# Pass one of a fused attention and two-layer kernel: block writes placed behind the raw loads, a third staging buffer, and a bank of its own for one product

## The chip, the cores and the metric

One core of one Trainium2 chip runs the whole program. The metric is device time in microseconds, from one launch. Engines are named as the profile names them: PE is TensorE (PEld its weight loads), DVE is VectorE, ACT is ScalarE, POOL is GpSimd, and SP is SyncE, which here only issues transfers (SPq).

## What is computed

Block-causal attention feeds a first feed-forward layer, whose output, after an RMS norm, feeds a gated second one.

```python
x = attention(q, k, v)              # 4 x 8 heads x 576 x 64 -> 2304 x 512
h = x @ w_in                        # 512 x 2048
x = (h - tanh(h)) @ w_out           # 2048 x 512
rms = sqrt(mean(x * x, -1) + 1e-06)
xn = x / rms * rms_g
g, val = xn @ w_gate, xn @ w_val    # 512 x 1536 each
out = (g / (1 + exp(-g)) * val) @ w_out2
```

All inputs arrive as 8-byte floats. The kernel converts them on the chip: a raw piece of 128x1024 words is loaded by SP into a staging tile `st` (`stage`, L125 to L131) and rebuilt into 128x512 floats by four instructions of `convert` (L133 to L145), two on ACT (L141, L143) and two on DVE (L144, L145).

## The kernel before

**Precision.** Every product of the feed-forward layers is made of three matmuls, high by high, high by low, low by high (L1068 to L1070 for the second layer's first half, L746 to L748 for output GEMMs). So each weight and each activation is kept as a rounded high part, made on ACT, and the rest, made on DVE (L108 is the helper's subtraction).

**The second layer** runs in three passes of 768 tokens (two groups of 384 that share a scheme). In a pass there are 12 blocks (`J2`) of 128 hidden columns of gate and value. A block is `fast` (L1101): seven products of six matmuls each in place of eight, in the order 1, 4, 5, 6, 0, 3, 2. Product 1 opens a bank, ACT copies it to `c11` (L1118), and product 0 is later added onto the same bank. DVE adds product 4 to `c11` (L1119, giving `u`), product 5 to `u` (L1120, `c12`), and product 6 to `c12` (L1122, `c22`). Product 6's bank is called `lower`; product 2, the seventh, is added onto it, so it can start only when L1122 has read `lower`. Then L1124 adds product 3, L1127 takes `lower` plus `u`, and L1128 multiplies with the silu; POOL multiplies the other result (L1126). Blocks 3 and 4 of pass one (`MIXED`) are `plain` (L1130), eight products without sums between them. After the twelfth block (j = 11) come seven output GEMMs (`tail`, L1189), whose left factors are split on ACT and DVE as they go.

**Where pass one's weights come from.** Passes two and three load a block's ready weights from DRAM (`w2d`). Pass one makes them as it goes. The steps for block n are: two raw pieces are loaded (`load`, two `stage` calls); each is converted into `fu` (`piece`); `fill` with half 0 splits the first three or four of the block's seven weight sums into a slot `ws` (ACT L801, DVE L108), then POOL forms the other sums in place (`sums`, L792 to L796), and `fill` with half 1 splits those; `keep` (L812 to L814) writes the filled slot to `w2d` for the later passes. For blocks 3 and 4, whose slot holds only the plain parts, `send` (L816 to L825) splits the second half into a tile `wc` and writes that. There are three slots, so the fill for block j + 3 waits until PE has finished block j and until the write of block j's slot has landed. The staging pool `st2` has two buffers: a raw load waits until ACT has read the piece two before it.

**What sets the order.** The engines' instruction order is fixed when the kernel is built, by a scheduler that follows modelled times, up to block 10 of pass one; from there on DVE, ACT and POOL follow the order in which the code is written. On the chip each engine runs its own list strictly in that order and waits on semaphores. All transfers here are issued by SP, in one list. A step j of pass one (L1297 to L1325) does in the order of the code: fill 0 of block j + 2; fill 1, `keep` and, for blocks 3 and 4, `send` of block j + 1; conversion of block j + 3's second piece; raw loads of block j + 4 and conversion of its first piece; then the products of block j.

Of the kernel before, what the change touches and what calls it, by code (L numbers as in the profile page):

```python
# [10 lines left out]
F32 = mybir.dt.float32  # L11
# [4 lines left out]
ALU = mybir.AluOpType  # L16
# [11 lines left out]
J2 = FF2 // 128  # L28
# [66 lines left out]
def build(ctx, tc, q, k, v, w_in, w_out, w_gate, w_val, w_out2, rms_g, ident_in, out):  # L95
    nc = tc.nc
    pin = tc.keep_in_program_order
# [18 lines left out]
    wod = drm.tile([128, 7, JH, 512], F32, name="wod")  # L116
# [475 lines left out]
    with tc.manual_schedule(engines={PE.engine}):  # L592
# [181 lines left out]
        class Convert:  # L774
# [38 lines left out]
                n = slice(0, 3 if self.j in MIXED else 7)  # L813
                pin(SP.dma_start(out=w2d[self.j][:, :, n], in_=self.w[:, :, n].bitcast(F32)))  # L814

            def send(self, half):  # L816

                n = slice(3, 7) if half else slice(0, 3)
                w = env["wc"]()[:, :, 0:n.stop - n.start]
                self.split_part(w)  # L820
                if self.kind == "g":
                    pin(SP.dma_start(out=w2d[self.j][:, :, n], in_=w.bitcast(F32)))
                    return
                for y in range(2):
                    pin(SP.dma_start(out=wod[:, n, self.j, 256 * y:256 * y + 256], in_=w[:, y].bitcast(F32)))  # L825

        def away(units, stay=(), raw=()):

# [103 lines left out]
        for s in range(NSA):  # L932
# [72 lines left out]
            if j == J1 - 1:  # L1005
                while att.pos < goal:
                    att.step()
                if g == NG - 2:
                    mid.__exit__(None, None, None)
                    evm.__exit__(None, None, None)  # L1010
                    cvs.__exit__(None, None, None)
                    x4.__exit__(None, None, None)
                    sat.close()
                    sw = ExitStack()
                    tp = sw.enter_context(tc.tile_pool(name="w2p", bufs=1, side="right"))
                    sw0 = ExitStack()
                    env["cvp"] = sw0.enter_context(tc.tile_pool(name="w0", bufs=1, side="right"))
                    env["stg"] = sw0.enter_context(tc.tile_pool(name="st2", bufs=2, side="right"))
                    sev = ExitStack()
                    ev = sev.enter_context(tc.tile_pool(name="ev", bufs=3, side="right"))  # L1020
                    space = tp.tile([128, 2, 7, 256], F32R, name="ws", tag="ws", bufs=3).bitcast(F32)
                    space = space.rearrange("p x n c -> p (x n c)")
                    env["x2s"] = lambda g, t: (space[:, DM * t:DM * t + DM] if g == NG - 2 else
                                               ev.tile([128, DM], F32, name="x2s", tag="x2s"))
                    x = pair_x()
                    wcp = sev.enter_context(tc.tile_pool(name="wcp", bufs=1, side="right"))
                    env["wc"] = lambda: wcp.tile([128, 2, 4, 256], F32R, name="wc", tag="wc")
                    direct = [Convert("g", j) for j in range(J2)]
                    items = away([direct[n] for n in (10, 0, 11, 1, 2, 3, 4)], direct[0:3], direct[3:5])
# [71 lines left out]
        def fast(s, j, x):  # L1101
# [4 lines left out]
            def prod(n, xx, m, onto=None):  # L1106
                ps = any_bank()[:, 0:TG] if onto is None else onto
                h, l = (y[:, 2 * m:2 * m + 2] for y in xx)
                product(ps, w[:, 0, n], w[:, 1, n], h, l, onto is None, True, onto is not None)
                return ps  # L1110
# [13 lines left out]
            DVE.tensor_tensor(c12, prod(3, xc, 1), c12, ALU.add)  # L1124
            ACT.activation(out=c12, in_=c12, func=AF.Silu)  # L1125
            POOL.tensor_tensor(out=result(1, j), in0=c12, in1=c22, op=ALU.mult)  # L1126
            DVE.tensor_tensor(c21, prod(2, xd, 0, lower), u, ALU.add)  # L1127
            DVE.tensor_tensor(result(0, j), c21, gt, ALU.mult)  # L1128

        def plain(s, j, x, xu):  # L1130
# [149 lines left out]
        def upper(j):  # L1280

            if j == 0:
                env["xu"] = tp.tile([128, 8, 256], F32, name="xn", tag="xn", bufs=2)
                for t in range(TT):
                    c = TT + t
                    SP.dma_start(out=env["xu"][:, t], in_=x2d[c * 128:(c + 1) * 128, 256:512])
            elif j == 1:
                for t in range(TT):
                    v, c = env["xu"][:, t], TT + t
                    ACT.activation(out=v, in_=v, func=AF.Copy, scale=rinv[:, c:c + 1])  # L1290
            elif j == 2:
                for t in range(TT):
                    turn(env["xu"][:, t], t, xu, bank())

        ordered = ExitStack()
        for p in range(NG // 2):
            for j in range(J2):  # L1297
                if p == 0 and j == WHOLE.stop:
                    ordered.enter_context(tc.manual_schedule(engines={DVE.engine, ACT.engine, POOL.engine}))
                if p or j:  # L1300
                    load_slot(p * NQ + j + 2)
                if p == 0:
                    if j + 1 in WHOLE:
                        direct[j + 1].fill(slots[j + 1], 1)
                    if j + 1 < WHOLE.stop:
                        direct[j + 1].keep()
                        if j + 1 in MIXED:
                            direct[j + 1].send(1)
                    if 5 <= j + 3 < WHOLE.stop:
                        direct[j + 3].piece(1)  # L1310
                    if 5 <= j + 4 < WHOLE.stop:
                        direct[j + 4].load()
                        direct[j + 4].piece(0)
                    upper(j)
                if j == J2 - 1:
                    ahead = splits()
# [39 lines left out]
```

## Time and profile before

| what | us |
|---|---|
| median of three runs | 1025.9 |
| lowest, highest | 1025.07, 1026.9 |
| the profiled execution, own time | 1026.08 |
| its span | 1023.2 |
| TensorE busy in it | 1005.7 (98%) |
| VectorE busy in it | 725.0 (71%) |
| pass one's blocks (first product of block 0 to that of block 11) | 605.7 to 691.7 |

The profiled execution's own time is 2.9 us over its span, and 0.18 us over the median. The granted clock of TensorE is 1.0 over the whole span. All times of day below are microseconds from the start of that span. In a timeline row the first number is the start, the second the duration, then engine, source line, operation, output tile <- input tiles, shape and count; in brackets stands the idle time of that engine before it and what ended it. Instructions of one engine may overlap a little, since the next starts while the last results of one drain.

### The profile page before, as it was taken

How to read it: one execution, taken by the hardware profiler on the slowest of the kernel's cores; microseconds unless marked ns; L12 is line 12 of the kernel's file. 1: busy time of each engine (PE TensorE's matmuls, PEld its weight loads, DVE VectorE, ACT ScalarE, POOL GpSimd, SP SyncE). 2: the span in 40 equal slices, each digit the busy share in tenths (PEclk: the TensorE clock that was granted, in tenths of full speed). 3: DMA queues.
4: the chain of work that ended last, by engine and by line, in shares of the span. 5: the costliest groups of instructions: out<-in, count | busy, mean ns of one | idle time of the engine just before them, and what ended most of it. 6: DMA issues, size and time to landing. Idle time of an engine off the chain costs nothing.

```text
span 1023.2 us, 17884 instructions
## 1 busy us (share of the span) xinstructions
PE 1005.7 (98%) x6001; PEld 924.5 (90%) x6001; DVE 725.0 (71%) x1492; ACT 663.9 (65%) x1534; POOL 344.9 (34%) x472
## 2 busy tenths in 40 slices
PE   8999999999999999999999999999999999999998
PEld 5767789998898899999999989999999999999998
DVE  6877867767777767677767888868865568645665
ACT  6988978778898877788858775625632247422253
POOL 6522102222324143344334425575121470112610
PEclk9999999999999999999999999999999999999999
DMA  9899959856787689867869989986796757866664
GB/s 230 260 352 346 294 171 270 246 162 178 199 221 180 187 236 315 218 202 258 280 209 371 384 322 341 346 336 237 287 339 248 255 218 267 299 267 248 236 240 131
DMA packets 186651, 265.61 MB, mean 260 GB/s; under 512 B 109120, under 2 KB 150848, under 8 KB 179520
## 3 DMA queue, kind: packets, MB, share of 16 engines
q1 hardware_dynamic: 185616, 264.22, 78.6%
q8 instruction: 47, 0.77, 0.3%
q10 hardware_dynamic: 944, 0.26, 0.1%
q14 instruction: 44, 0.36, 0.1%
HBM read 202.05 MB, written 62.39 MB: 258 GB/s over the span
## 4 chain that ended last, share of the span: by engine, by line
PE 83%; DVE 3%; ACT 2%; DMA 2%; issue 1%; SPq 0%; POOL 0%; DVEq 0%; POOLq 0%
PE t L715 6%; PE t L716 5%; PE t L717 5%; PE acc L746 5%; PE acc L748 5%; PE gv L1068 5%; PE gv L1070 5%; PE acc L747 5%; PE gv L1069 5%; PE t L481 5%; PE t L525 3%; PE ga L1070 3%; PE ga L1069 3%; PE ga L1068 3%; PE ga L748 3%; PE ga L746 2%
## 5 line engine op out<-in xcount | busy, mean ns | idle before, releaser
L715 PE MATMUL t<-xh,w 128*128 128x384 f32 x384 | 137.7, 359 | 0.3
L717 PE MATMUL t<-xh,w 128*128 128x384 f32 x384 | 129.8, 338 | 0.4 <-DVE w L108 0.3
L716 PE MATMUL t<-xl,w 128*128 128x384 f32 x384 | 129.4, 337 | 0.7 <-POOL xl L108 0.7
L1068 PE MATMUL gv<-xh,ws 128*128 128x384 f32 x314 | 105.8, 337 | 2.3 <-DVE vb L1122 2.3
L1070 PE MATMUL gv<-xh,ws 128*128 128x384 f32 x314 | 105.6, 336 | 0.1
L1069 PE MATMUL gv<-xl,ws 128*128 128x384 f32 x314 | 105.4, 336 | 0.0
L746 PE MATMUL acc<-w,gh 128*128 128x512 f32 x252 | 103.1, 409 | 0.2 <-ACT gh L103 0.2
L748 PE MATMUL acc<-w,gl 128*128 128x512 f32 x252 | 99.6, 395 | 0.3 <-DVE gl L108 0.3
L747 PE MATMUL acc<-w,gh 128*128 128x512 f32 x252 | 99.1, 393 | 0.0
L496 ACT ACTIVATE pt<-pt,stat 128x64 f32<-128x64 f32 (+2 forms) x144 | 80.2, 558 | 25.1 <-DVE pt L494 24.2
L1126 POOL TENSOR_TENSOR g<-va,vb 128x384 f32<-128x384 f32 x34 | 36.0, 1058 | 149.1 <-ACT va L1125 132.6
L715 PEld LDWEIGHTS t<-xh,w 128*128 128x128 f32 x384 | 72.3, 188 | 5.7 <-issue 1.2
L716 PEld LDWEIGHTS t<-xl,w 128*128 128x128 f32 x384 | 72.4, 189 | 3.7 <-POOL xl L108 1.0
L494 DVE TENSOR_SCALAR_CACHE_REDUCE pt<-t 128x64 f32<-128x64 f32 (+2 forms) x144 | 63.9, 448 | 13.2 <-PE t L481 12.1
L717 PEld LDWEIGHTS t<-xh,w 128*128 128x128 f32 x384 | 72.0, 188 | 1.0 <-DVE w L108 1.0
L986 DVE TENSOR_TENSOR gt<-t,gt 128x384 f32<-128x384 f32 x84 | 46.3, 551 | 32.4 <-ACT gt L980 32.1
L108 DVE TENSOR_TENSOR gl<-gt,gh 128x384 fp32r<-128x384 f32 x84 | 55.7, 663 | 17.1 <-ACT gh L103 16.8
L525 PE MATMUL t<-ident,pt 128*128 128x128 f32 x400 | 64.6, 273 | 1.7 <-POOL pt L510 1.6
L108 DVE TENSOR_TENSOR pp<-t,pp 128x512 fp32r<-128x512 f32 (+3 forms) x112 | 55.3, 508 | 14.6 <-ACT pp L103 13.9
L103 ACT ACTIVATE pp<-t 128x512 fp32r<-128x512 f32 (+5 forms) x144 | 60.4, 437 | 7.3 <-PE t L525 6.7
L1070 PE MATMUL ga<-xh,ws 128*128 128x384 f32 x186 | 62.6, 336 | 1.3 <-DVE ws L108 1.3
L1068 PE MATMUL ga<-xh,ws 128*128 128x384 f32 x186 | 62.6, 337 | 0.0
(208 smaller groups left out, 2988.9 us busy)
## 6 DMA issues: line engine op xcount, KB each, us to landing
ws<-w2d SPq DMA_DIRECT2D x26, 1792.0 KB, 7.4
ws<-wod SPq DMA_DIRECT2D x21, 1536.0 KB, 6.3
w<-w1d_i SPq DMA_DIRECT2D x60, 512.0 KB, 5.0
w<-w1d_o SPq DMA_DIRECT2D x48, 512.0 KB, 4.7
st<-in_moe_w_out SPq DMA_DIRECT2D x28, 512.0 KB, 6.0
w2d<-ws SPq DMA_DIRECT2D x8, 1792.0 KB, 8.8
st<-in_moe_w_in SPq DMA_DIRECT2D x16, 512.0 KB, 6.1
w1d_i<-w SPq DMA_DIRECT2D x16, 512.0 KB, 6.2
```

The lines of the kernel that those rows point to most:

```text
L108: eng.tensor_tensor(out=o, in0=full, in1=hi.bitcast(F32), op=ALU.subtract)
L496: ACT.activation(out=pt[:, 0:keys], in_=pt[:, 0:keys], func=AF.Exp, scale=-1.0, bias=least, accum_out=st[:, 8 + ti:9 + ti])
L525: PE.transpose(t[:, (j - a) * 128:(j - a + 1) * 128], pt[:, j * 128:(j + 1) * 128], ident)
L715: PE.matmul(h, lhsT=wh[:, c], rhs=xh[:, kk], start=(kk == 0), stop=False)
L716: PE.matmul(h, lhsT=wh[:, c], rhs=xl[:, kk], start=False, stop=False)
L717: PE.matmul(h, lhsT=wl[:, c], rhs=xh[:, kk], start=False, stop=(kk == KD - 1))
L746: PE.matmul(acc, lhsT=gh[:, c], rhs=wh, start=first, stop=False, skip_group_check=more)
L747: PE.matmul(acc, lhsT=gh[:, c], rhs=wl, start=False, stop=False, skip_group_check=more)
L748: PE.matmul(acc, lhsT=gl[:, c], rhs=wh, start=False, stop=last, skip_group_check=more)
L1068: PE.matmul(ps, lhsT=wh[:, c], rhs=xh[:, kk], start=(first and kk == 0), stop=False, skip_group_check=more)
L1069: PE.matmul(ps, lhsT=wh[:, c], rhs=xl[:, kk], start=False, stop=False, skip_group_check=more)
L1070: PE.matmul(ps, lhsT=wl[:, c], rhs=xh[:, kk], start=False, stop=(last and kk == nk - 1), skip_group_check=more)
```

## The change

Three edits. First, the writes of pass one's step (`keep`, and the write half of `send`) are collected in a list and issued after the step's raw loads; `send` is cut into `apart`, which splits on ACT and DVE and returns its write, and the write itself. Second, the staging pool `st2` has three buffers where it had two. Third, in `fast`, for the twelfth block of every pass, product 2 opens a bank of its own (the counter `nbank` takes one more step per pass), and two DVE additions take the place of one. The matmuls are the same in number and, but for the banks' names, in order; DVE has one instruction more in each pass.

```diff
--- before.py
+++ after.py
@@ -813,16 +813,22 @@
                 n = slice(0, 3 if self.j in MIXED else 7)
                 pin(SP.dma_start(out=w2d[self.j][:, :, n], in_=self.w[:, :, n].bitcast(F32)))
 
-            def send(self, half):
+            def apart(self, half):
 
                 n = slice(3, 7) if half else slice(0, 3)
                 w = env["wc"]()[:, :, 0:n.stop - n.start]
                 self.split_part(w)
-                if self.kind == "g":
-                    pin(SP.dma_start(out=w2d[self.j][:, :, n], in_=w.bitcast(F32)))
-                    return
-                for y in range(2):
-                    pin(SP.dma_start(out=wod[:, n, self.j, 256 * y:256 * y + 256], in_=w[:, y].bitcast(F32)))
+
+                def write():
+                    if self.kind == "g":
+                        pin(SP.dma_start(out=w2d[self.j][:, :, n], in_=w.bitcast(F32)))
+                        return
+                    for y in range(2):
+                        pin(SP.dma_start(out=wod[:, n, self.j, 256 * y:256 * y + 256], in_=w[:, y].bitcast(F32)))
+                return write
+
+            def send(self, half):
+                self.apart(half)()
 
         def away(units, stay=(), raw=()):
 
@@ -1015,7 +1021,7 @@
                     tp = sw.enter_context(tc.tile_pool(name="w2p", bufs=1, side="right"))
                     sw0 = ExitStack()
                     env["cvp"] = sw0.enter_context(tc.tile_pool(name="w0", bufs=1, side="right"))
-                    env["stg"] = sw0.enter_context(tc.tile_pool(name="st2", bufs=2, side="right"))
+                    env["stg"] = sw0.enter_context(tc.tile_pool(name="st2", bufs=3, side="right"))
                     sev = ExitStack()
                     ev = sev.enter_context(tc.tile_pool(name="ev", bufs=3, side="right"))
                     space = tp.tile([128, 2, 7, 256], F32R, name="ws", tag="ws", bufs=3).bitcast(F32)
@@ -1124,7 +1130,11 @@
             DVE.tensor_tensor(c12, prod(3, xc, 1), c12, ALU.add)
             ACT.activation(out=c12, in_=c12, func=AF.Silu)
             POOL.tensor_tensor(out=result(1, j), in0=c12, in1=c22, op=ALU.mult)
-            DVE.tensor_tensor(c21, prod(2, xd, 0, lower), u, ALU.add)
+            if j == J2 - 1:
+                DVE.tensor_tensor(c21, lower, u, ALU.add)
+                DVE.tensor_tensor(c21, prod(2, xd, 0), c21, ALU.add)
+            else:
+                DVE.tensor_tensor(c21, prod(2, xd, 0, lower), u, ALU.add)
             DVE.tensor_tensor(result(0, j), c21, gt, ALU.mult)
 
         def plain(s, j, x, xu):
@@ -1300,17 +1310,20 @@
                 if p or j:
                     load_slot(p * NQ + j + 2)
                 if p == 0:
+                    writes = []
                     if j + 1 in WHOLE:
                         direct[j + 1].fill(slots[j + 1], 1)
                     if j + 1 < WHOLE.stop:
-                        direct[j + 1].keep()
+                        writes.append(direct[j + 1].keep)
                         if j + 1 in MIXED:
-                            direct[j + 1].send(1)
+                            writes.append(direct[j + 1].apart(1))
                     if 5 <= j + 3 < WHOLE.stop:
                         direct[j + 3].piece(1)
                     if 5 <= j + 4 < WHOLE.stop:
                         direct[j + 4].load()
                         direct[j + 4].piece(0)
+                    for write in writes:
+                        write()
                     upper(j)
                 if j == J2 - 1:
                     ahead = splits()
```

In the changed file the lines of `fast` stand a few lines lower: L1125, L1126, L1128, L1130, L1137, L1138 are the former L1119, L1120, L1122, L1124, L1127, L1128; `xlu` parts (a transposed quarter of the activations) are made at L903 instead of L897, and `plain`'s multiply is L1155 instead of L1145. L108, L144 and L145 are as before. The list moves as well, because the scheduler sees other times. Three places on DVE follow.

VectorE between the last instruction of block 1 and block 2's `c22` sum, before. Here `gv` and `ga` are banks, `fu` float pieces, `cv` and `cu` conversion temporaries; `ws_7925` is the slot of block 4, `wc_7933` the second half of block 3.

```order
L897 TENSOR_TENSOR xlu_7771<-gv_7954,xhu_7770 128x2x128
L897 TENSOR_TENSOR xlu_7771<-gv_7959,xhu_7770 128x2x128
L897 TENSOR_TENSOR xlu_7771<-gv_7964,xhu_7770 128x2x128
L1119 TENSOR_TENSOR va_7970<-gv_7981,c11_7969 128x384
L1120 TENSOR_TENSOR va_7970<-gv_7989,va_7970 128x384
L108 TENSOR_TENSOR ws_7925<-fu_7640,ws_7925 128x1024
L1122 TENSOR_TENSOR vb_7971<-ga_7997,va_7970 128x384
L108 TENSOR_TENSOR wc_7933<-fu_7547,wc_7933 128x1024
L144 TENSOR_SCALAR cv_7853<-cv_7853 128x512
L1124 TENSOR_TENSOR va_7970<-ga_8012,va_7970 128x384
L144 TENSOR_SCALAR cv_7937<-cv_7937 128x512
L145 SCALAR_TENSOR_TENSOR fu_7852<-cv_7853,cu_7854 128x512
```

The same place after, where `wc_7932` is the second half of block 3:

```order
L108 TENSOR_TENSOR ws_7925<-fu_7640,ws_7925 128x1024
L108 TENSOR_TENSOR wc_7932<-fu_7547,wc_7932 128x1024
L144 TENSOR_SCALAR cv_7935<-cv_7935 128x512
L903 TENSOR_TENSOR xlu_7771<-gv_7954,xhu_7770 128x2x128
L145 SCALAR_TENSOR_TENSOR fu_7851<-cv_7852,cu_7853 128x512
L903 TENSOR_TENSOR xlu_7771<-gv_7959,xhu_7770 128x2x128
L145 SCALAR_TENSOR_TENSOR fu_7851<-cv_7935,cu_7936 128x512
L903 TENSOR_TENSOR xlu_7771<-gv_7964,xhu_7770 128x2x128
L1125 TENSOR_TENSOR va_7970<-gv_7981,c11_7969 128x384
L144 TENSOR_SCALAR cv_7946<-cv_7946 128x512
L1126 TENSOR_TENSOR va_7970<-gv_7989,va_7970 128x384
L1128 TENSOR_TENSOR vb_7971<-ga_7997,va_7970 128x384
```

Before, two fills (L108) and a conversion step stand between block 2's additions, and only the first of them ahead of `vb` (L1122). Now both fills, L144 and two L145 stand ahead of block 2's first addition and another L144 ahead of its second; `vb` (L1128) is the twelfth.

VectorE between block 4's last product and block 5's `vb`, before; `ws_8208` is the slot of block 7 and `ws_8121` that of block 6.

```order
L1145 TENSOR_TENSOR g1_4_8206<-ga_8193,gt_8178 128x384
L144 TENSOR_SCALAR cv_8131<-cv_8131 128x512
L145 SCALAR_TENSOR_TENSOR fu_8054<-cv_8131,cu_8132 128x512
L1119 TENSOR_TENSOR va_8236<-gv_8247,c11_8235 128x384
L108 TENSOR_TENSOR ws_8208<-fu_8054,ws_8208 128x768
L1120 TENSOR_TENSOR va_8236<-gv_8255,va_8236 128x384
L108 TENSOR_TENSOR ws_8121<-fu_7947,ws_8121 128x1024
L1122 TENSOR_TENSOR vb_8237<-gv_8263,va_8236 128x384
```

After:

```order
L1155 TENSOR_TENSOR g1_4_8206<-ga_8193,gt_8178 128x384
L108 TENSOR_TENSOR ws_8208<-fu_8052,ws_8208 128x768
L108 TENSOR_TENSOR ws_8121<-fu_7945,ws_8121 128x1024
L144 TENSOR_SCALAR cv_8217<-cv_8217 128x512
L145 SCALAR_TENSOR_TENSOR fu_8140<-cv_8141,cu_8142 128x512
L1125 TENSOR_TENSOR va_8236<-gv_8247,c11_8235 128x384
L145 SCALAR_TENSOR_TENSOR fu_8140<-cv_8217,cu_8218 128x512
L1126 TENSOR_TENSOR va_8236<-gv_8255,va_8236 128x384
L144 TENSOR_SCALAR cv_8228<-cv_8228 128x512
L1128 TENSOR_TENSOR vb_8237<-gv_8263,va_8236 128x384
```

The two fills now come ahead of block 5's first addition, and three more conversion steps stand between them and `vb` (L1128). Block 6 reads alike, with the fills of 8 and 7, one L144 and two L145 ahead of its `vb`.

VectorE in block 7, before; `ws_8298` is the slot of block 8, `ws_8377` that of block 9.

```order
L1119 TENSOR_TENSOR va_8388<-gv_8399,c11_8387 128x384
L144 TENSOR_SCALAR cv_8229<-cv_8229 128x512
L1120 TENSOR_TENSOR va_8388<-gv_8407,va_8388 128x384
L145 SCALAR_TENSOR_TENSOR fu_8228<-cv_8229,cu_8230 128x512
L144 TENSOR_SCALAR cv_8308<-cv_8308 128x512
L1122 TENSOR_TENSOR vb_8389<-gv_8415,va_8388 128x384
L145 SCALAR_TENSOR_TENSOR fu_8228<-cv_8308,cu_8309 128x512
L1124 TENSOR_TENSOR va_8388<-ga_8430,va_8388 128x384
L108 TENSOR_TENSOR ws_8377<-fu_8228,ws_8377 128x768
L1127 TENSOR_TENSOR vb_8389<-gv_8415,va_8388 128x384
L108 TENSOR_TENSOR ws_8298<-fu_8141,ws_8298 128x1024
L1128 TENSOR_TENSOR g0_7_8448<-vb_8389,gt_8390 128x384
```

After:

```order
L108 TENSOR_TENSOR ws_8377<-fu_8227,ws_8377 128x768
L108 TENSOR_TENSOR ws_8298<-fu_8140,ws_8298 128x1024
L1125 TENSOR_TENSOR va_8388<-gv_8399,c11_8387 128x384
L1126 TENSOR_TENSOR va_8388<-gv_8407,va_8388 128x384
L1128 TENSOR_TENSOR vb_8389<-gv_8415,va_8388 128x384
L1130 TENSOR_TENSOR va_8388<-ga_8430,va_8388 128x384
L1137 TENSOR_TENSOR vb_8389<-gv_8415,va_8388 128x384
L1138 TENSOR_TENSOR g0_7_8448<-vb_8389,gt_8390 128x384
```

The second half of block 8's weights, which stood behind block 7's L1127, now stands ahead of block 7's first addition, and no conversion is left in block 7.

On SP, block 1's write is in its place of before (behind the three stores `x2d`), but blocks 5 and 6 have had three more raw pieces issued ahead of it; block 2's write has moved behind block 4's and 5's raw loads, block 3's behind the second piece of block 6.

## Rows read from the trace of the kernel before

**Rows 1.** One 100-us window: us, PE busy (x), PEld, DVE, ACT, POOL, PEclk, DMA share, GB/s.

```profile
600.00:700.00 100.00, 96.97 (x542) 93.70 (x541) 79.92 (x118) 52.04 (x93) 53.84 (x52) 1.00 0.90 334
```

**Rows 2.** TensorE's waits, whole span: engine line <- releaser: total us, times, longest.

```profile
PE gv L1068 <- DVE vb L1122: 2.3, 2, 1.1
...
PE ga L1070 <- DVE ws L108: 1.3, 1, 1.3
...
PE acc L748 <- DVE gl L108: 0.3, 1, 0.3
```

**Rows 3.** TensorE timeline, blocks 7 and 8: start us, us, engine line.

```profile
661.18 0.33 PE L1068 MATMUL gv<-xh,ws 128*128 128x384 f32 x1
...
662.60 0.33 PE L1068 MATMUL gv<-xh,ws 128*128 128x384 f32 x1
...
669.03 0.44 PE L1068 MATMUL ga<-xh,ws 128*128 128x384 f32 x1
...
671.78 0.33 PE L1068 MATMUL gv<-xh,ws 128*128 128x384 f32 x1
```

**Rows 4.** VectorE timeline, the late second half of block 8's weights.

```profile
669.41 1.51 DVE L108 TENSOR_TENSOR ws<-fu,ws 128x1024 fp32r<-128x1024 f32 x1
```

**Rows 5.** TensorE timeline, block 2's first and seventh product; blocks 5, 6.

```profile
621.14 0.42 PE L1068 MATMUL gv<-xh,ws 128*128 128x384 f32 x1
...
627.51 0.33 PE L1068 MATMUL ga<-xh,ws 128*128 128x384 f32 x1
...
645.40 0.34 PE L1068 MATMUL ga<-xh,ws 128*128 128x384 f32 x1
...
652.80 0.34 PE L1068 MATMUL gv<-xh,ws 128*128 128x384 f32 x1
```

**Rows 6.** VectorE timeline, blocks 0 to 2: conversions, splits and chain.

```profile
611.58 0.42 DVE L144 TENSOR_SCALAR cv<-cv 128x512 f32<-128x512 f32 x1
...
612.13 0.69 DVE L145 SCALAR_TENSOR_TENSOR fu<-cv,cu 128x512 int32<-128x512 int32 x1
...
617.67 1.23 DVE L108 TENSOR_TENSOR ws<-fu,ws 128x1024 fp32r<-128x1024 f32 x1 [0.73 <-ACT ws L801]
...
621.43 1.28 DVE L1128 TENSOR_TENSOR g<-vb,gt 128x384 f32<-128x384 f32 x1
...
622.64 1.07 DVE L897 TENSOR_TENSOR xlu<-gv,xhu 128x256 fp32r<-128x256 f32 x3
...
626.64 1.51 DVE L108 TENSOR_TENSOR wc<-fu,wc 128x1024 fp32r<-128x1024 f32 x1
...
628.08 0.96 DVE L144 TENSOR_SCALAR cv<-cv 128x512 f32<-128x512 f32 x1
...
629.84 1.22 DVE L145 SCALAR_TENSOR_TENSOR fu<-cv,cu 128x512 int32<-128x512 int32 x1
```

**Rows 7.** GpSimd timeline beside them.

```profile
626.34 0.73 POOL L792 TENSOR_TENSOR fu<-fu 128x256 f32<-128x256 f32 x1 [3.02 <-DVE ws L108]
...
627.15 1.61 POOL L793 TENSOR_TENSOR fu<-fu 128x256 f32<-128x256 f32 x1
```

**Rows 8.** TensorE timeline, block 11 of passes one and three.

```profile
696.88 0.33 PE L1068 MATMUL gv<-xh,ws 128*128 128x384 f32 x1
...
699.22 0.44 PE L1068 MATMUL gv<-xh,ws 128*128 128x384 f32 x1 [1.14 <-DVE vb L1122]
...
972.17 0.44 PE L1068 MATMUL gv<-xh,ws 128*128 128x384 f32 x1 [1.13 <-DVE vb L1122]
```

**Rows 9.** VectorE timeline at the end of pass one's block 11.

```profile
700.59 0.56 DVE L1127 TENSOR_TENSOR vb<-gv,va 128x384 f32<-128x384 f32 x1 [0.76 <-PE gv L1070]
...
704.47 1.37 DVE L108 TENSOR_TENSOR gl<-g,gh 128x384 fp32r<-128x384 f32 x1
```

**Rows 10.** TensorE timeline, the first GEMM behind it.

```profile
705.97 0.31 PE L748 MATMUL ga<-ws,gl 128*128 128x256 f32 x1
```

**Rows 11.** DMA issue of block 1's write: KB, us to landing.

```profile
w2d<-ws SPq DMA_DIRECT2D x1, 1792.0 KB, 14.6
```

## Prediction

> **What bounds the kernel now.** I read the 100-us windows first, then TensorE's waits, then the timelines of the engines that end those waits. TensorE is the bound: from 600 to 700 us, where pass one's blocks lie, it is busy for 96.97 of 100 us at a granted clock of 1.00 [rows 1]. So the change can win only what TensorE still waits for there, and the list of waits is short [rows 2]: 1.3 us once for the low half of a weight slot (`ws`, L108), 2.3 us in two waits for `vb` (L1122), and 0.3 us for `gl` at the end of the first layer. Against that, DVE is busy for 79.92 of the 100 us, far more than ACT or POOL [rows 1]. DVE makes the low parts, and it also does the additions that free the banks. Where its list puts one ahead of the other decides who waits.
>
> Starts of products give the losses in full, since a wait row leaves out the refilling of the pipeline. A product of six matmuls takes 1.05 us (696.88 to 697.92 if nothing is late; six of them fill 621.14 to 627.51 with 0.1 lost) [rows 5, 8]. In block 8, product 4 starts at 669.03 and the next at 671.78: 2.75 us, so 1.70 lost, because the second half of block 8's weights is split only from 669.41, for 1.51 us [rows 3, 4]. In block 7 the same distance is 1.42 (661.18 to 662.60): 0.37 lost [rows 3]. With 0.15 ahead of 669.03 the late fills cost 2.2 us. In block 11 of passes one and three product 2 waits for `vb` and starts at 699.22 in place of 697.92, 1.3 us late; the wait at 972.17 is as long [rows 8].
>
> **The writes and the third buffer: what goes.** Raw pieces come earlier, so conversions and fills do too. The order shows it: block 8's second half is split ahead of block 7's first addition, some five us earlier against the products. All 2.2 us of late fills should go: **-2.2**. If the raw loads did not come in time, none of it would: 0 is the other end. At the end of the first layer one conversion step leaves the stretch in which TensorE waits 0.3 us [rows 2], but another L144 and L145 still stand ahead of the last `gl`: **-0.2** (0 to -0.5).
>
> **What comes instead.** The moved work is now bunched on DVE ahead of the block's chain, and that chain has a due time: product 2, the block's seventh, is added onto `lower`, and can start only when `vb` has read it. Block 2 first. Its product 2 is due at 627.51 [rows 5]. Block 1's last DVE instruction starts at 621.43; bare it takes 0.56, as its like do [rows 6, 9], so DVE is free at 622.0. Then follow, one behind the other, two fills at 1.23, L144 at 0.42 twice, the three `xlu` at 1.07 together, two L145 at 0.69, and three additions at 0.56 [rows 6, 9]: 2.46 + 0.84 + 1.07 + 1.38 + 1.68 = 7.4 us. Neighbours overlap by 0.07 (626.64 plus 1.51 against 628.08 [rows 6]), eleven times, which leaves 6.7. So `vb` is done at 628.7 at the earliest, and TensorE waits 1.2 us.
>
> That is the bare price, and these instructions seldom get it. POOL starts its four sums when the first fill is done, 0.73 us each when alone [rows 7], and while they run the DVE instructions with both inputs in SBUF get longer: the fill 1.51 in place of 1.23, L145 1.22 for 0.69, L144 0.96 for 0.42, the multiply L1128 1.28 for 0.56 [rows 6]; the sums too, 1.61 [rows 7]. Instructions that read a bank don't change. If a fill, one L144 and both L145 are hit, that is 0.28 + 0.54 + 1.06 = 1.9 more, and half a us more if block 1's last one is hit as well: a wait of 3.6. Four sums cannot meet everything; I take the middle, **+2.5** (1.2 to 3.6).
>
> Block 5 starts at 645.40, so its product 2 is due at 651.7 [rows 5]. DVE is free at 646.3, behind ACT's high part of the first fill, which waits for block 4's last product. A fill of 768 columns (some three quarters of 1.23) and one of 1024, two L144, two L145 and three additions come to 0.95 + 1.23 + 0.84 + 1.38 + 1.68 - 8 x 0.07 = 5.5: `vb` at 651.8, 0.1 late, and up to 2.6 with what POOL adds. Again the middle: **+1.4**. Block 6 starts at 652.80 [rows 5], product 2 due at 659.1. The last instruction of block 5 ends at 654.2, two additions behind its last product; the same run with one L144 fewer takes 5.1: 659.3, so 0.2 late, and up to 3.0. The order gives it one SBUF instruction fewer to meet the sums, so below the middle: **+1.1**. Block 7 has two fills and no conversion left, and block 8 one fill: `vb` comes in time by a us or more. Blocks 3 and 4 have no such chain. Sum of the new waits: **+5.0** (1.5 to 9). Nothing hides them, as TensorE's next product needs that bank and its list is fixed.
>
> **The skill on this sharing.** The Trainium skill, page "SBUF — State Buffer", section "Who interferes with whom", says that a DVE instruction with two SBUF inputs contends with a GpSimd one that reads SBUF, and that the first holds the shared pair "for the whole instruction; the other fully blocks (not throttle)". The rows agree in kind (L1128's 1.28 is 0.56 plus some 0.7). Taken to its end it speaks against this change: each such instruction behind the first fill would wait out a whole sum; that is the third rival.
>
> **The bank.** For the twelfth block product 2 no longer waits for `vb`: 1.3 us each in passes one and three. But DVE's list does not get shorter. Ahead of L1127 it idles 0.76 us for that product [rows 9]; the new addition of 0.56 fills just this idle time, so the chain ends as before. The first output GEMM runs at the pace of DVE's splits: the split that starts at 704.47 takes 1.37 and ends at 705.84, and TensorE uses it at 705.97 [rows 9, 10]. A TensorE that comes 1.3 us earlier waits there, all but 0.13. So -0.1 each. Pass two has no such wait [rows 2], only the new addition, 0 to 0.56: I take +0.1. Together **-0.1** (-2.6 if the splits follow TensorE, +0.5 at worst).
>
> **Sum.** -2.2 - 0.2 + 5.0 - 0.1 = +2.5. On the profiled execution, 1026.08, that is 1028.6 us. The median of the runs lies 0.18 lower: 1028.4, rounded down, since I rather overrate the meeting with POOL, to **1028.3**.
>
> **Rivals.**
> - *About the same.* DVE gets through near the bare prices: waits of 1.2 + 0.1 + 0.2 to 2.5 in all, and they eat the gain. -2.2 - 0.2 + 2.5 - 0.1 = 0: 1025.9. For it: half of DVE's instructions read a bank. Against: POOL's sums start exactly with this run.
> - *Faster.* The bank edit gives its 2.6 in full. It needs the splits to be earlier too, which the 0.76 us of idle DVE time speaks against, and the bare prices besides: -2.2 - 0.2 + 2.5 - 2.6 = -2.5: 1023.4.
> - *Full turns with POOL.* Every run waits out all four sums of 0.73 in whole, 3.0 us over bare: 4.2 + 3.1 + 3.2 = 10.5, so +8.0: 1033.9. Against: a fill beside them grew by 0.28 only [rows 6], so most instructions meet part of a sum.
> - *The write comes too late.* Block 1's write is issued at 608.10 and lands 14.6 us later, at 622.7 [rows 11]; block 4's first fill needs its slot, and this fill now leads the run in block 2. If the write stays as late, the run starts at 623.8, 1.8 later than above: +4.3, 1030.2. The Trainium skill, "DMA: Bandwidth & Descriptors", section "Queues, rings and completion order", has each DMA engine take its descriptors in ring order, so three raw pieces more ahead would count against it. For an earlier landing speaks that the order lets those pieces and block 0's write out earlier than before; I expect it before 621.
> - *It doesn't do what it says:* raw loads still wait for ACT's reading, the late fills stay, and the bunching stays too. That is slower than the forecast by 2.2, at 1030.5, and shares the chance of the late write.
>
> **How the numbers follow.** Two tenths of a per cent, about what a measurement of this kernel can tell from none, is 2.05 us: faster is below 1023.85, slower above 1027.95. Chances: the forecast 0.47 (its own range 1026.9 to 1030.5), about the same 0.24, faster 0.13, full turns 0.07, late write or late loads 0.09. A third of the forecast's own chance lies below 1027.95, so "same" has 0.24 + 0.16 = 0.40, and slower 0.31 + 0.16 = 0.47. The range leaves out most of the faster case and the full turns: 1024.3 to 1031.4.
>
> **What would show it.** In the trace of after: no TensorE wait for `ws` in blocks 7 and 8; waits of 1 us or more for L1128 (the former L1122) at product 2 of blocks 2, 5 and 6, with two fills and L145 ahead of it on DVE; at block 11's product 2 no wait, but one for `gl` or `va` (L108) in the first GEMM. The forecast is wrong if blocks 2, 5 and 6 keep the length of before, or if the first GEMM starts and runs 1.3 us earlier.

## The result, and the profile after

The changed kernel takes 1034.11 us in the median of five runs (1032.49 to 1038.54), the kernel before 1025.9 beside it. The medians lie 8.2 us apart; the ratio is 1.0089, with a 95% interval of 1.0071 to 1.0107, which makes it 9.1 us slower (7.3 to 11.0), outside the range that was given. The direction was right, the size was not.

| | before | after |
|---|---|---|
| median of five runs, us | 1025.9 | 1034.11 |
| profiled execution, us | 1026.08 | 1038.54 |
| its span, us | 1023.2 | 1036.7 |
| TensorE's mean granted clock | 1.0 | 0.994 |

The profiled execution of the changed kernel is 4.4 us over its median. 3.9 us of that lie in the first 135 us, where no instruction moved: TensorE waits 3.7 us there for `pt`, where it waited 1.1 before, and then runs for some 3.5 us at a granted clock of 0.50 (half clock, in what follows). From there until the first layer's end every matmul stands 3.9 us later than its like in the trace before. In the traces of the runs below this offset lies anywhere between -0.6 and 4.5 us. So all comparisons here are made by offsets: the start of a matmul minus the start of the same matmul before, and what matters is where the offset grows.

The window that answers to [rows 1], shifted by the 3.9 us:

```profile
604.00:704.00 100.00, 91.91 (x496) 88.64 (x496) 72.19 (x108) 49.10 (x87) 50.52 (x48) 0.97 0.80 303
```

TensorE is busy for 91.91 us where it was for 96.97, and its granted clock is 0.97 where it was 1.00. The waits of TensorE (engine line <- releaser: us in total, times, longest) that answer to [rows 2]:

```profile
PE acc L746 <- DMA w<-w1d_o: 2.5, 1, 2.5
PE gv L1074 <- DVE xlu L903: 2.4, 1, 2.4
PE ga L1074 <- DVE vb L1128: 1.4, 1, 1.4
PE gv L1074 <- DVE vb L1128: 1.4, 1, 1.4
PE ga L748 <- DVE va L108: 0.7, 1, 0.7
...
PE ga L746 <- DVE va L1130: 0.4, 1, 0.4
```

The 1.3 us for `ws` and the 2.3 us for `vb` in block 11 are gone. New are 2.5 us for a weight load of the *first* layer (`w1d_o`), 2.4 us for `xlu`, and the two waits of 1.4 us in blocks 5 and 6. The timeline of TensorE at these places (start, duration):

```profile
607.97 0.39 PE L748 MATMUL acc<-w,gl 128*128 128x512 f32 x1
610.84 0.47 PE L746 MATMUL acc<-w,gh 128*128 128x512 f32 x1 [2.48 <-DMA w<-w1d_o]
...
613.95 0.52 PE L1074 MATMUL gv<-xh,ws 128*128 128x384 f32 x1
...
634.50 0.44 PE L1074 MATMUL gv<-xh,ws 128*128 128x384 f32 x1 [2.38 <-DVE xlu L903]
...
666.06 0.44 PE L1074 MATMUL gv<-xh,ws 128*128 128x384 f32 x1 [1.37 <-DVE vb L1128]
...
675.11 0.44 PE L1074 MATMUL ga<-xh,ws 128*128 128x384 f32 x1 [1.45 <-DVE vb L1128]
```

The row at 613.95 shows something else: a matmul that takes 0.34 us elsewhere takes 0.52. Two-us windows of the same trace (the last three columns are granted clock, DMA share, GB/s) say why:

```profile
608.00:610.00 2.00, 0.36 (x2) 0.00 (x0) 1.83 (x4) 1.14 (x3) 0.00 (x0) 1.00 0.89 240
...
612.00:614.00 2.00, 2.00 (x7) 1.52 (x6) 1.06 (x2) 1.25 (x4) 0.00 (x0) 0.50 1.07 451
614.00:616.00 2.00, 2.00 (x10) 2.00 (x9) 1.01 (x2) 1.73 (x3) 0.00 (x0) 0.68 0.89 358
...
636.00:638.00 2.00, 2.00 (x8) 2.00 (x7) 2.00 (x5) 0.57 (x1) 1.00 (x1) 0.50 1.03 410
```

Behind each of the two long waits TensorE ran for some 3.5 us at a granted clock of 0.50, the lower of its two levels (1.2 GHz). The whole account, by offsets against the trace before:

| stretch | offset, us | change |
|---|---|---|
| up to the first layer's last steps | 3.9 | |
| first layer's end, waits for ACT and DVE | 5.6 | +1.7 |
| its last output weights | 7.9 | +2.3 |
| before's own wait for `gl` gone, then half clock; then, by the end of block 1, 0.2 that only the trace before had lost | 8.6 | -0.6, +1.5, -0.2 |
| block 2: wait for `xlu`, then half clock | 12.8 | +2.5, +1.7 |
| block 5 | 14.4 | +1.6 |
| block 6 | 16.1 | +1.7 |
| blocks 7 and 8: late fills gone | 13.9 | -2.2 |
| block 11 and first GEMM, pass one: -1.4, then +1.4 | 13.9 | 0.0 |
| the other GEMMs of pass one, and pass two | 14.0 | +0.1 |
| block 11 and first GEMM, pass three: -1.4, then +1.4 | 14.0 | 0.0 |
| the rest of pass three | 13.6 | -0.4 |

13.6 less 3.9 is 9.7 us, within the interval of the timed runs. The last 0.4 is not the change's: every trace below falls by it in that stretch, those without the bank edit too. And the account is of this one execution, with a mean granted clock of 0.994. The other four have 0.997 or 0.998, so they ran less at half clock.

### The profile page after: what moved, and what is told of

Read it like the earlier page. It is cut to its first block, busy times and chain, and to the rows that moved or that the text cites. A ratio compares the mean times of both kernels' runs of the same rounds, so it can differ in the third digit from the quotient of the medians.

```text
span 1036.7 us, 17905 instructions
## 1 busy us (share of the span) xinstructions
PE 1011.0 (98%) x6001; PEld 928.5 (90%) x6001; DVE 727.2 (70%) x1495; ACT 662.7 (64%) x1534; POOL 347.3 (33%) x472
## 4 chain that ended last, share of the span: by engine, by line
PE 72%; ACT 8%; DMA 7%; DVE 7%; issue 2%; SPq 2%; POOL 1%; DVEq 0%; ACTq 0%; POOLq 0%
PE gv L1074 5%; PE gv L1076 5%; PE gv L1075 5%; PE t L481 5%; PE acc L746 4%; PE t L715 4%; PE acc L748 4%; PE acc L747 4%; PE t L716 4%; PE t L717 4%; PE t L525 3%; PE ga L1074 3%; PE ga L1076 3%; PE ga L1075 3%; PE ga L748 3%; PE t L550 2%
## 5 line engine op out<-in xcount | busy, mean ns | idle before, releaser
L1074 PE MATMUL gv<-xh,ws 128*128 128x384 f32 x318 | 107.6, 338 | 3.7 <-DVE xlu L903 2.4
L1076 PE MATMUL gv<-xh,ws 128*128 128x384 f32 x318 | 107.2, 337 | 0.0
L494 DVE TENSOR_SCALAR_CACHE_REDUCE pt<-t 128x64 f32<-128x64 f32 (+2 forms) x144 | 63.8, 447 | 13.6 <-PE t L481 12.5
L108 DVE TENSOR_TENSOR gl<-gt,gh 128x384 fp32r<-128x384 f32 x84 | 55.2, 657 | 15.7 <-ACT gh L103 15.4
L108 DVE TENSOR_TENSOR pp<-t,pp 128x512 fp32r<-128x512 f32 (+3 forms) x112 | 55.3, 508 | 14.6 <-ACT pp L103 13.9
L525 PEld LDWEIGHTS t<-ident,pt 128*128 128x128 f32 x400 | 50.4, 141 | 16.1 <-POOL pt L510 5.2
L1074 PEld LDWEIGHTS gv<-xh,ws 128*128 128x128 f32 x318 | 60.3, 190 | 4.5 <-DVE xlu L903 2.7
```

The lines of the kernel that those rows point to most:

```text
L108: eng.tensor_tensor(out=o, in0=full, in1=hi.bitcast(F32), op=ALU.subtract)
L525: PE.transpose(t[:, (j - a) * 128:(j - a + 1) * 128], pt[:, j * 128:(j + 1) * 128], ident)
L1074: PE.matmul(ps, lhsT=wh[:, c], rhs=xh[:, kk], start=(first and kk == 0), stop=False, skip_group_check=more)
L1076: PE.matmul(ps, lhsT=wl[:, c], rhs=xh[:, kk], start=False, stop=(last and kk == nk - 1), skip_group_check=more)
```

## Experiments

**One part alone.** Three kernels are the one before with one of the three edits each. The third edit:

```diff
+            if j == J2 - 1:
+                DVE.tensor_tensor(c21, lower, u, ALU.add)
+                DVE.tensor_tensor(c21, prod(2, xd, 0), c21, ALU.add)
+            else:
...
```

> The kernel before with the third edit alone (product 2 of block 11 in a bank of its own). My theory: the wait of 1.3 us ahead of that product goes in passes one and three, and the first output GEMM gives 1.0 to 1.4 us of each back in waits for VectorE's splits, so the time changes by 0 to -0.6 us: 1025.3 to 1025.9. Rival: the splits follow TensorE and all 2.6 us are won: 1023.3.

Measured: 1025.22 us beside 1025.58, ratio 0.9995 (0.9983 to 1.0006): no change that can be told. The trace shows both halves. Product 2 comes 1.30 us earlier in pass one, against the matmuls ahead of it, and the first GEMM gives all of it back, beginning with

```profile
703.50 0.39 PE L748 MATMUL ga<-ws,va 128*128 128x256 f32 x1 [0.74 <-DVE va L108]
```

At the end of pass one the offset is what it was ahead of block 11 (0.2), and so it is behind the first GEMM of pass three. From there to the end it falls by 0.4 us, but it does so as well in buf and writes, which lack this edit. The theory holds: the splits on VectorE set the pace there.

The second edit:

```diff
-                    env["stg"] = sw0.enter_context(tc.tile_pool(name="st2", bufs=2, side="right"))
+                    env["stg"] = sw0.enter_context(tc.tile_pool(name="st2", bufs=3, side="right"))
```

> The kernel before with the second edit alone (three staging buffers, writes in their old place in the code). My theory: the third buffer alone makes the new order, since VectorE's list comes out as in the changed kernel and block 0's write stands ahead of the first layer's last output weights on SyncE. So it has the whole loss: a TensorE wait of 2 to 3 us for those weights, one of some 2.5 us in block 2, 1.4 to 1.6 us each in blocks 5 and 6, and half clock for some 3.5 us behind each of the two longer ones; 1033 to 1036. Rival: the loss comes from the writes behind the loads; then 1024 to 1027 here.

Measured: 1034.83 us beside 1025.58, ratio 1.0074 (1.0049 to 1.0100). TensorE's waits are those of the changed kernel, and block 11's of before:

```profile
PE gv L1068 <- DVE vb L1122: 3.6, 3, 1.4
PE acc L746 <- DMA w<-w1d_o: 2.6, 1, 2.6
...
PE gv L1068 <- DVE xlu L897: 2.4, 1, 2.4
```

The offset grows by 4.7 us at the first layer's end, 4.2 in block 2, 1.6 and 1.7 in blocks 5 and 6, and falls by 2.2 with the late fills. So one more buffer, without the writes' move, is enough for the whole loss; on VectorE the list is the changed kernel's but for block 11.

The first edit alone is the diff's `writes` list and `apart`, with two buffers:

```diff
-                        direct[j + 1].keep()
+                        writes.append(direct[j + 1].keep)
...
+                    for write in writes:
+                        write()
```

> The kernel before with the first edit alone (writes behind the raw loads, two staging buffers). My theory: no loss, since block 0's write stays behind the first layer's last weights and VectorE's list keeps fills and additions mixed in blocks 2, 5 and 6; the late second half of block 8's weights stays or gets worse, as it now stands behind block 7's last instruction: 1025 to 1027.5. Rival: the loss comes from this edit: 1030 or more, with the wait for the last weights.

Measured: 1033.26 us beside the same 1025.58, ratio 1.0074 (1.0049 to 1.0100). The theory failed here; the rival has the size right but not the place. The last weights of the first layer do come in time (the offset is 4.5 before and behind that layer's end), so that part of the theory stands. But the offset grows by 2.0 us in blocks 0 and 1, 3.6 in block 5 and 2.4 in blocks 7 and 8. I had looked at VectorE's list, and the longest new waits come from ScalarE:

```profile
PE ga L1074 <- ACT c L1124: 1.9, 1, 1.9
...
PE ga L1076 <- DVE ws L108: 1.2, 1, 1.2
...
PE gv L1074 <- ACT c L1124: 1.0, 1, 1.0
...
PE ga L1074 <- ACT ws L801: 0.6, 1, 0.6
```

The wait for `ws` (L108) is the late fill of block 8, which stays, as expected. Behind the wait of 1.9 us in block 5 and behind that late fill TensorE runs at half clock, which is about 1.5 us of the growth each time. ScalarE's timeline at the two places, in blocks 0 and 5:

```profile
612.79 0.66 ACT L141 ACTIVATE cv<-st 128x512 f32<-128x512 f32 x1 [2.39 <-DMA st<-in_moe_w_val]
...
615.06 0.49 ACT L1124 ACTIVATE c<-gv 128x384 f32<-128x384 f32 x1
...
655.87 1.79 ACT L801 ACTIVATE ws<-fu 128x768 fp32r<-128x768 f32 x2 [2.92 <-DVE fu L145]
657.57 0.47 ACT L1124 ACTIVATE c<-ga 128x384 f32<-128x384 f32 x1
```

In both, the copy of product 1 to `c11` (L1124) stands behind a conversion or fill that waits, for a raw piece or for VectorE; product 0 can't start before that copy. This is read from the timelines; no run took the two conversions away. So the first edit costs about as much alone as the second, by another way, and the two losses don't add, since together they give the second one's list.

**The last weights.** The changed kernel with one line moved:

```diff
-                if j == 14:
-                    direct[0].keep()
...
+        direct[0].keep()
         rms(12, 18)
```

> The changed kernel with one line moved: block 0's write is issued behind the loop of the first layer, and so behind that layer's last output weights on SyncE. My theory: those weights land in time, the TensorE wait of 2.5 us and the half clock behind it go (-4 to -5 us against the changed kernel); VectorE's list in blocks 1 and 2 changes with it (the three xlu ahead of the fills), so most of block 2's loss of 4 us goes too: 1025 to 1028. Blocks 5 and 6 keep their waits of 1.5 us each. Rival: the weights are late because three more raw pieces are in flight, whatever the write's place; then the wait stays at 2 us or more and the time at 1030 or more.

Measured: 1028.96 us, ratio 1.0031 (1.0018 to 1.0044), some 5 us less than the changed kernel. The wait for `w1d_o` and the half clock behind it are gone. That layer's lists on ScalarE and VectorE are unchanged up to there, so SyncE's list is the cause. The last weight load (KB, us from issue to landing) in the kernel before, the changed kernel, and this one:

```profile
w<-w1d_o SPq DMA_DIRECT2D x1, 512.0 KB, 7.7
```

```profile
w<-w1d_o SPq DMA_DIRECT2D x1, 512.0 KB, 13.3
```

```profile
w<-w1d_o SPq DMA_DIRECT2D x1, 512.0 KB, 8.5
```

The changed kernel issues it 1.4 us behind block 0's write of 1792 KB and 2 us behind a raw piece. Against the other transfers it is issued only 1.2 us later than before (597.43 less the offset of 3.9 is 593.5, before it was 592.37); what stands in front of it makes it late. The Trainium skill, "DMA: Bandwidth & Descriptors", section "Queues, rings and completion order", has each DMA engine take descriptors in ring order, and these rows agree. The offset grows here by 0.8 us up to block 2, 1.0 in block 2, 2.1 in block 5 and 1.1 in block 6, and falls by 2.2. So the waits for ACT and DVE at the layer's end and a rest in block 2 stay, and the time lies 1 us above what I expected.

**Block 2: which instruction, or the whole run.** The prediction had TensorE wait for `vb` there. In the changed kernel it waits already at product 5, whose bank is still held by a transposed piece of activations until `xlu` has been read. VectorE's list there:

```profile
630.06 0.91 DVE L1138 TENSOR_TENSOR g<-vb,gt 128x384 f32<-128x384 f32 x1
630.90 1.22 DVE L108 TENSOR_TENSOR ws<-fu,ws 128x1024 fp32r<-128x1024 f32 x1
632.03 1.21 DVE L108 TENSOR_TENSOR wc<-fu,wc 128x1024 fp32r<-128x1024 f32 x1
633.17 0.95 DVE L144 TENSOR_SCALAR cv<-cv 128x512 f32<-128x512 f32 x1
634.03 0.41 DVE L903 TENSOR_TENSOR xlu<-gv,xhu 128x256 fp32r<-128x256 f32 x1
...
638.10 0.56 DVE L1128 TENSOR_TENSOR vb<-ga,va 128x384 f32<-128x384 f32 x1
```

`vb` ends at 638.66. Block 2 starts at 629.77, so product 2 would have been due at 636.14: 2.5 us late even if product 5 had not waited. To tell the two apart, the transposes go ahead of the fills:

```diff
+                if p == 0 and j == 2:
+                    upper(j)
                 if p or j:
                     load_slot(p * NQ + j + 2)
...
```

> The changed kernel with block 2's transposes placed ahead of that step's fills in the code, so that the three xlu stand ahead of the two fills on VectorE; from L1128 (vb) of block 2 on, and on SyncE and TensorE, the lists are unchanged. My theory (the length of VectorE's run decides, not the one instruction that TensorE meets first): the wait of 2.4 us for xlu at product 5 goes and comes back as a wait for vb at product 2, 2.0 to 2.6 us, since the same instructions stand ahead of vb; block 2 stays about as long. Rival (the bank held by the transposes is the cause): no wait over 0.5 us in block 2, and with it no half clock, some 4 us less. The wait for the first layer's last weights stays in both.

One execution, with these waits:

```profile
PE ga L1074 <- DVE vb L1128: 3.9, 2, 2.4
...
PE acc L746 <- DMA w<-w1d_o: 1.3, 1, 1.3
```

The wait moved as the theory has it: none for `xlu`, and 2.42 us for `vb` at product 2, with 2.8 us of offset. Freeing one bank earlier wins nothing. (The execution took 1032.26 us. There was no half clock in it; more on that below.)

**What draws the run out.** GpSimd's sums for blocks 4, 7 and 8 run beside VectorE's bunched runs in blocks 2, 5 and 6. This kernel leaves them out:

```diff
-                    self.sums()
+                    if self.j not in (4, 7, 8):
+                        self.sums()
```

> The changed kernel without GpSimd's four sums for blocks 4, 7 and 8 (those blocks' weights are therefore wrong), which are the sums that run beside VectorE's bunched runs in blocks 2, 5 and 6; the lists of all other engines are unchanged. My theory (VectorE's instructions with two SBUF inputs are drawn out by GpSimd): L108, L144 and L145 there take their bare 1.21, 0.42 and 0.69 us, the waits for vb in blocks 5 and 6 fall from 1.4 to 0.0 to 0.3 us, block 2's from 2.4 to 1.2 to 2.0 us. Rival (the run is simply too long): the waits stay within 0.3 us of what they are.

One execution, of 1026.69 us. The start of block 5's run in the changed kernel, and then in this one:

```profile
661.42 0.96 DVE L144 TENSOR_SCALAR cv<-cv 128x512 f32<-128x512 f32 x1
662.30 1.22 DVE L145 SCALAR_TENSOR_TENSOR fu<-cv,cu 128x512 int32<-128x512 int32 x1
...
665.46 0.55 DVE L1128 TENSOR_TENSOR vb<-gv,va 128x384 f32<-128x384 f32 x1
```

```profile
652.05 0.42 DVE L144 TENSOR_SCALAR cv<-cv 128x512 f32<-128x512 f32 x1
652.39 0.69 DVE L145 SCALAR_TENSOR_TENSOR fu<-cv,cu 128x512 int32<-128x512 int32 x1
...
654.86 0.55 DVE L1129 TENSOR_TENSOR vb<-gv,va 128x384 f32<-128x384 f32 x1
```

From L144's start to `vb`'s start it is 4.04 us with the sums and 2.81 without. The losses in blocks 5 and 6 fall from 1.6 and 1.7 us to 0.3 and 0.6, block 2's wait from 2.38 to 1.85. So some seven tenths of the losses in blocks 5 and 6 come from GpSimd's sums, and the rest from the bunching itself. L144 has one input in SBUF and grows all the same, from 0.42 to 0.96. The Trainium skill, "SBUF — State Buffer", section "Who interferes with whom", counts `tensor_scalar` among the operations that can take the pair of ports shared with GpSimd. The rows agree: without the sums L144 is back at 0.42.

**An order without the losses.** On top of keep0_late, pass one's conversions go behind the products in the code:

```diff
-                    if 5 <= j + 3 < WHOLE.stop:
-                        direct[j + 3].piece(1)
...
                     fast(p * NQ + j, j, x)
+                if p == 0:
+                    if 5 <= j + 3 < WHOLE.stop:
+                        direct[j + 3].piece(1)
...
```

> The changed kernel with block 0's write behind the first layer (as in keep0_late) and, in pass one, the conversions of a step placed behind its products in the code; raw loads, fills and writes stay where they are. On VectorE at most two fills and one L144 then stand ahead of vb in blocks 5 and 6. My theory: the waits for vb in blocks 5 and 6 fall from 1.9 and 0.8 us (keep0_late) to under 0.3, the late fill of block 8 stays away, and against the kernel before the late fills (2.2 us) are won and some 1 us is lost at the first layer's end: 1024 to 1026. Rival (conversions that start later make the fills late again): TensorE waits of over 1 us for ws (L108) in blocks 6 to 9, 1027 or more.

Measured: 1027.35 us, ratio 1.0019 (1.0009 to 1.0029). Blocks 5 and 6 lose 0.3 and 0.0 us, and the late fills stay away (-2.2), as the theory has it. The time doesn't follow, because the order makes other waits:

```profile
PE gv L1073 <- DVE xlu L903: 1.1, 1, 1.1
...
PE gv L1073 <- DVE vb L1127: 1.0, 1, 1.0
```

The second is in block 8, where the fill of block 9's second half, which waits for its sums, stands ahead of `vb`. At the first layer's end 0.7 us are lost as well. The last kernel is meant to mend these three:

```diff
-                while len(items) > max(24 * (J1 - 2 - j) // (J1 - 1), 0):
+                while len(items) > max(24 * (J1 - 2 - j) // (J1 - 1), 2):
...
             DVE.tensor_tensor(c22, lower, c12, ALU.add)
+            if s == 8:
+                direct[9].fill(slots[9], 1)
+                direct[9].keep()
...
+                if p == 0 and j == 2:
+                    upper(j)
...
```

> All three edits of the changed kernel, with the order mended where the runs found losses: block 0's write behind the first layer, conversions behind the products (both as in pieces_last), block 2's transposes ahead of its fills, the last two conversions of block 4 in block 0 in place of the end of the first layer, and block 9's second half filled behind block 8's vb. My theory: the three losses that pieces_last still has go (1.0 us at the first layer's end, 1.1 for xlu in block 2, 1.1 for vb in block 8), the 2.2 us of late fills stay won, and the bank gives some 0.3: 1023 to 1025, the kernel before being 1025.5. Rival: raw pieces that are converted later make block 4's or 5's fills late, and a wait of 1 us or more appears for ws or c11 in blocks 3 to 6: 1026 or more.

Measured: 1026.85 us beside 1026.11, ratio 1.0014 (1.0004 to 1.0024). Still not faster, and the theory failed: the first layer's end still loses 0.7 us, and block 2 now 1.9 where it lost 1.4. The offset falls by 1.3 through blocks 7 and 8, and grows by 0.8 for a load that now comes too late:

```profile
PE ga L1073 <- DVE vb L1127: 0.8, 1, 0.8
PE ga L1073 <- DMA ws<-w2d: 0.8, 1, 0.8
```

The second line is block 11's slot, behind block 9's postponed write. Behind the first GEMM the offset is 1.1 us, as it was ahead of that wait. No order tried here beats the kernel before; the best of them gains the 2.2 us and loses some 3 elsewhere.

## Why the prediction failed, point by point

- *Late fills, -2.2.* Right: the offset falls by 2.2 us in blocks 7 and 8 of the changed kernel, and by as much in buf, keep0_late, turn_first, nosums and pieces_last.
- *First layer's end, -0.2 (0 to -0.5).* Wrong, and the largest miss: +4.7 us. The step looked only at DVE's list ahead of the last `gl`, and counted one conversion less. It did not walk SyncE's list there. On it block 0's write had moved ahead of the first layer's last output weights: +2.3, and +1.5 at half clock behind it, shown by keep0_late. And conversions moved into that stretch as well as out of it, on ACT too: 1.7 us of waits and of refilling behind them. That this comes from the conversions is read from the lists; no run shows it by itself, and in mended, where the last two of them left the stretch, the 1.7 us stayed (0.7 net of the waits that the trace before has there). My late-transfer rival had the right mechanism at the wrong transfer: block 1's write, which nobody waited for.
- *Block 2, +2.5.* The size was right to a tenth (2.5), the place was not: TensorE met the bank held for `xlu` first. turn_first shows that the run's length, which the sum had added up, sets it either way. The bare length was right as well: from the end of block 1's multiply to that of `vb` it is 6.7 us in nosums, as added up. That the middle between the ends hit so well is in part luck. In the changed kernel the sums draw the run out by 1.0 of the 1.9 us that it allowed for them, and the multiply (L1138) ends 0.35 later than bare. That last part has nothing to do with the sums: it takes 0.91 with them and, in nosums, without. The 1.28 of [rows 6] was misread, as it lies for the most part beside GpSimd's own multiply, here in the kernel before:

```profile
621.29 1.01 POOL L1126 TENSOR_TENSOR g<-va,vb 128x384 f32<-128x384 f32 x1
```

- *Blocks 5 and 6, +1.4 and +1.1.* They cost 1.6 and 1.7. The bare ends of 0.1 and 0.2 were near what nosums shows (0.3, 0.6), and the lengths under GpSimd's sums (0.96, 1.22) were those of [rows 6]. Taking block 6 below the middle had no good ground, and its upper end of 3.0 doesn't follow from its terms (0.2 + 1.9 + 0.5 is 2.6).
- *Full turns with GpSimd.* It did not come to that. L144 and L145 grow by 0.54 and 0.53 us, about three quarters of a sum of 0.73 [rows 7], and in block 5 only the first of each kind does: the second L145 takes 0.76, the second L144 0.48. In block 2 both L145 take 0.9.
- *The clock.* Not in the sum at all. Two waits of 2.4 to 2.5 us brought 1.5 and 1.7 us at half clock on top, 3.2 us together. The trace before has a clock of 1.00 over this stretch and no wait over 1.4 us, so it held no row for this price.
- *The bank, -0.1 (-2.6 to +0.5).* Right: 0.0 in pass one and in pass three of the bank kernel's trace, and not to be told from no change in its time. The reason given is the one seen. The +0.1 for pass two doesn't show.

The sum in the prediction was +2.5; with the layer's end at +4.7 in place of -0.2, block 2's half clock at +1.7 and the rest as measured it comes to 9.7. Half of the gap of 7.2 us is one transfer and the clock that fell behind it, a quarter is block 2's half clock.

## What to carry to other kernels

When a buffer is added or a write is moved, walk the issuing engine's whole list over the stretch in which it changed, and ask of each load that someone waits for which bytes now stand in front of it: a write of 1.8 MB delayed a load by 5.6 us although it was issued hardly later. Work that comes earlier has to stand somewhere: in a list that is fixed at build time it stands in front of something, on ScalarE and SyncE as well as on the engine one looks at. And give a new wait of TensorE of some two us a price and a chance for a stretch at half clock behind it: here it came behind five of the eight waits of 1.85 us or more in the first layer's end and pass one, and cost 1.3 to 1.7 us each time.

## What the runs showed of the hardware

The same wait does not always bring the clock down. In the changed kernel and in buf, waits of 2.38 to 2.58 us were followed by a granted clock of 0.50, four times out of four; in writes, one of 1.89 was too, and one of 1.23 that had waits of 0.44 and 0.60 us in the five us ahead of it:

```profile
681.93 0.44 PE L1076 MATMUL ga<-xh,ws 128*128 128x384 f32 x1 [1.23 <-DVE ws L108]
```

```profile
684.00:686.00 2.00, 2.00 (x8) 2.00 (x7) 0.56 (x1) 1.06 (x1) 0.81 (x2) 0.50 0.93 373
```

In turn_first one of 2.42 us was not:

```profile
630.00:632.00 2.00, 0.21 (x2) 0.00 (x0) 2.00 (x4) 1.22 (x2) 1.75 (x2) 1.00 1.05 405
632.00:634.00 2.00, 1.36 (x8) 1.37 (x9) 1.15 (x4) 0.54 (x2) 0.12 (x1) 1.00 0.99 310
634.00:636.00 2.00, 2.00 (x13) 2.00 (x12) 1.97 (x3) 2.00 (x3) 0.90 (x1) 1.00 0.88 329
```

nor, in keep0_late, one of 1.89, nor, in nosums, one of 1.85. What tells them apart was not settled. The wait for the last weights is not steady either: with the same order of transfers around it, it was 2.48, 2.58, 1.25 and 1.18 us in four executions (the changed kernel, buf, turn_first, nosums), and the clock fell in the first two alone. The load took 12.9 to 13.3 us in all four, but in the last two it was issued some 0.9 us earlier against the matmuls. The timed runs point the same way: of the five of buf, the two with a mean granted clock of 1.000 took 1031.15 and 1031.95 us, the three with 0.996 or 0.997 took 1034.83 to 1035.66. So the runs with such stretches and those without lie some 3 to 4 us apart here; the length of the wait itself may have a share in that.
